# Re-planning the start of a fused attention and mixer kernel: TensorE transposes, GpSimd copies of V, single PSUM banks, row-tiled terms and zero products

## The chip, the cores and the metric

The kernel runs on one core of one Trainium2 chip. The metric is the device time of one execution in microseconds (us). Five engines share the work: TensorE (PE in the profile; its weight loads are PEld), VectorE (DVE), ScalarE (ACT), GpSimd (POOL) and SyncE (SP), with 16 DMA engines beside them. Each result below is the median of several executions, with the lowest and highest. The span is the time from the first to the last traced instruction of one execution; the time is 1.7 to 1.9 us longer than the span of the same execution.

## The reference

Attention over 4 batches, 8 heads, 768 positions and head size 64, with 8 global columns, a causal local window of 96 and a linear position bias, is followed by a low-rank token mixer and a two-layer channel network. Everything is float32 outside; the kernel works in float16 inside.

```python
keep = is_global | is_local                    # 8 global columns, 96 local ones
scores = np.where(keep, q @ k.T / 8 + bias, -1e9)
a = softmax(scores)
x = concat_heads(a @ v)                        # (4, 768, 512)
h = x.transpose(0, 2, 1) @ U @ V               # U: 768x32, V: 32x768
u = x + h.transpose(0, 2, 1)
out = u + np.maximum(u @ w_ch1, 0.0) @ w_ch2   # 512x2048, 2048x512
```

## The kernel before

Two heads of one batch make a pair, so there are 16 pairs, four in each batch. Batch 0 is pairs 0 to 3. A pair is loaded, its q and k are transposed, 128-column blocks of scores are formed and exponentiated, and multiplied with V. Since the window crosses block boundaries, the kernel holds k and V a second time, shifted by one block, as kO and vo (with the 8 global rows in front). Then the mixer makes uT of the pair. When four pairs are done, TensorE runs the channel products of that batch: M1 is the first (128 matmuls of 384 columns in each batch) and M2 the second. The attention of the next batch is slotted between them.

Every piece is a task with an assumed duration, a priority and dependences. A planner in the kernel's own Python simulates the engines with these durations and fixes each engine's order of instructions before the kernel is built. An engine then runs its instructions strictly in that order.

```python
PRIO = {"E012": 1443.3, "EX1.1": 338.0, ...}   # hand-found priorities of single tasks

# loads: all are issued by GpSimd, in the order k, q, v of each pair
tk = add(POOL, ldur, ..., ld(stgk, k, gk), after=prev, ...)
tq = add(POOL, ldur, ..., ld(stgq, q, gq), after=tk, ...)
tv = add(POOL, 1.04, ..., ldv, [c_zero], after=tq, ...)

# transposes: batch 0 by TensorE, all later pairs by DMA
if first:
    TK = add(PE, 0.38, base, tr(g1, stgk, gk), ...)          # 12 matmuls with an identity
    EK = add(ACT, 0.83, base + 1, evac(kT, gkT, g1, ACT), ...)
else:
    EK = add(SP, 0.35, base + 1, dtr(kT, gkT, stgk, gk), ...)  # dma_start(..., transpose=True)

# shifted V: batch 0 by DMA, all later pairs by VectorE
if eng == SP:
    nc.sync.dma_start(vof[32:P], vv[32:P, :, 0:NB - 1])
    for hi in range(2):
        nc.sync.dma_start(vof[0:NG, hi], vv[0:NG, hi, 0:1].broadcast_to((NG, NB - 1, D1)))
else:
    nc.vector.tensor_copy(vof, vv[:, :, 0:NB - 1])
    nc.vector.tensor_copy(vof[0:32], vv[0:32, :, 0:1].broadcast_to((32, 2, NB - 1, D1)))

# mixer: an aligned pair of PSUM banks; U products in 32-column tiles, h over all 128 rows
gx = Group("ps", n=2, among=A2)
nc.tensor.matmul(ps[R * g:R * g + R, gx.slot, 384:512], u16[:, c], xx[:, c], ...)
nc.tensor.matmul(ps[:, gx.slot + half, 0:HS], tmp[...], vrep[:, half * HS:(half + 1) * HS], ...)
# cast of x for the mixer: GpSimd for three of a batch's four pairs
XC = add(POOL, 0.83, base + 22, cast, [NM], acq=[gx16], ...)
...   # cut: scores, softmax, channel products, stores
```

The softmax here doesn't subtract the row's maximum and nothing guards it: scores larger than these inputs give would overflow.

Of the kernel before, what the change touches and what calls it, by code (L numbers as in the profile page):

```python
# [20 lines left out]
    "E012": 1443.3, "EX1.1": 338.0, "KO11": 1058.2, "NH3.1": 393.2, "PV2.1": 317.9, "PV9.2": 1009.0,  # L21
    "S0.0": -8.2, "S1.1": -12.6, "S11.1": 970.6, "S13.2": 1162.2, "S14.0": 1415.1, "S2.0": 228.3,
    "S3.1": 286.5, "S3.2": 282.8, "S4.0": 363.6, "S4.2": 398.6, "S5.0": 533.1, "TE6": 676.1,
    "X02": 262.7, "X06": 650.3, "mask1": 377.5, "mask2": 223.5, "mask4": 285.4, "mask7": 304.8,
}
CFG = {}
# [19 lines left out]
class Planner:  # L46
# [4 lines left out]
    def __init__(self, counts, dma_rate, hold):  # L51
        self.tasks, self.names = [], {}
        self.free = {k: [0.0] * n for k, n in counts.items()}
        self.dma_rate, self.hold = dma_rate, hold
# [9 lines left out]
    def pick(self, g):  # L64
        free = self.free[g.kind]
        best = None
        for i in g.among if g.among is not None else range(0, len(free) - g.n + 1, g.n):
            f = max(free[i:i + g.n])
            if f < 1e8 and (best is None or f < best[0]):
                best = (f, i)  # L70
        return best

    def run(self):
# [28 lines left out]
        while len(order) < len(self.tasks):  # L102
            best = None
            for e in engines:
                ready = []
                for t, r in live[e].items():
                    for g in t.acq:
                        if g.slot is None:
                            got = self.pick(g)
                            if got is None:  # L110
                                break
                            r = max(r, got[0])
                    else:
                        if t.size:
                            r = max(r, lanes[e][t.parts - 1])
                        ready.append((max(r, clock[e]), t.prio, t))
# [12 lines left out]
            if t.size:  # L129

                begin = max(t.end + 1.5, dma_free[t.eng])
# [6 lines left out]
                t.end += 0.4  # L138
# [4 lines left out]
            for g in t.acq:  # L143
                if g.slot is None:
                    g.slot = self.pick(g)[1]
                    for i in range(g.slot, g.slot + g.n):
                        self.free[g.kind][i] = 1e9
            for g in t.rel:
                g.readers -= 1
                g.free_at = max(g.free_at, t.end + 0.1)  # L150
                if g.readers == 0:
                    for i in range(g.slot, g.slot + g.n):
                        self.free[g.kind][i] = g.free_at
            order.append(t)
# [9 lines left out]
def kernel(  # L164
# [36 lines left out]
    def sb(name, shape, dt, n=None):  # L201
# [4 lines left out]
    ident = sb("ident", [P, P], FP32)  # L206
    ident16 = sb("ident16", [P, P], FP16)
    reli = sb("reli", [P, 256], I32)
    relb = sb("relb", [P, 256], FP32)
    rel3 = sb("rel3", [P, 384], FP32)  # L210
    mask = sb("mask", [P, H, 384], FP16)
    bias = sb("bias", [P, H, 384], FP16)
    uf = sb("uf", [P, NB, R], FP32)
    u16 = sb("u16", [P, NB, R], FP16)
# [26 lines left out]
        dma_rate=0.30e6,  # L241
# [3 lines left out]
    def add(eng, dur, prio, fn, deps=(), name="", **kw):  # L245
        return pl.add(name, eng, dur, PRIO.get(name, prio), fn, deps, **kw)

    ANY1, ANY2 = None, None
# [4 lines left out]
    c_ident = add(POOL, 0.6, -50, lambda: make_identity(nc, ident), name="ident")  # L253
    c_id16 = add(DVE, 0.35, -50, lambda: nc.vector.tensor_copy(ident16, ident), [c_ident], name="id16")
    c_iota = add(
        POOL, 0.35, -52,
        lambda: nc.gpsimd.iota(reli, pattern=[[1, 256]], base=0, channel_multiplier=-1), name="iota",
    )
    c_relf = add(DVE, 0.36, -51, lambda: nc.vector.tensor_scalar_mul(relb, reli, -1.0), [c_iota], name="relf")

    def causal():
        nc.gpsimd.affine_select(
            out=relb, in_=relb, compare_op=ALU.is_ge, fill=BIG,
            base=0, pattern=[[1, 256]], channel_multiplier=-1,
        )

    def window():
        nc.gpsimd.affine_select(
            out=relb, in_=relb, compare_op=ALU.is_ge, fill=BIG,
            base=NL - 1, pattern=[[-1, 256]], channel_multiplier=1,  # L270
        )

    c_sel1 = add(POOL, 0.41, -49, causal, [c_relf], name="sel1")
    c_sel2 = add(POOL, 0.41, -48, window, [c_sel1], name="sel2")

    def build_rel():
        nc.vector.tensor_copy(rel3[:, 128:256], relb[:, 128:256])
        nc.vector.tensor_copy(rel3[:, 256:384], relb[:, 0:128])
        nc.vector.tensor_copy(rel3[:, 0:128], relb[:, 0:128])
        nc.vector.tensor_scalar_max(rel3[0:NG, 0:256], rel3[0:NG, 0:256], float(-NL))  # L280

    c_rel = add(DVE, 0.97, -46, build_rel, [c_sel2], name="rel3")
# [18 lines left out]
    for h in range(H):  # L301
        e = ACT if h >= 1 else DVE
        c_bias.append(add(e, 0.54, -45 + h if h < 2 else 100 * (h // 2) - 30, bias_of(h, e), [c_rel], name=f"bias{h}"))

    def zero_fill():
        for i in range(N_V):
            nc.vector.memset(vo[i][0:32], 0.0)
            nc.vector.memset(vt[i][:, :, :, D:D1], 1.0)

    c_zero = add(DVE, 1.0, -60, zero_fill, name="zero")  # L310
# [3 lines left out]
    loads, c_w1, c_w2 = {}, [], []  # L314

    def add_load(p):
# [5 lines left out]
        def ld(dst, src, g):  # L322
            def go():
                if b == 0:
# [15 lines left out]
        ldur, parts = (0.72, 1) if b == 0 else (1.7, 2)  # L340
        lead = 60 if b == 0 else 160
        prev = loads[p - 1][5] if p else None
        tk = add(POOL, ldur, base - lead, ld(stgk, k, gk), after=prev, acq=[gk], size=0.39e6, parts=parts, name=f"lk{p}")
        tq = add(POOL, ldur, base - lead + 1, ld(stgq, q, gq), after=tk, acq=[gq], size=0.39e6, parts=parts, name=f"lq{p}")
        tv = add(POOL, 1.04, base - lead + 2, ldv, [c_zero], after=tq, acq=[gv], size=0.39e6, name=f"lv{p}")
        loads[p] = (gq, gk, gv, tq, tk, tv)

    def add_w1(i, prio):
# [4 lines left out]
                after=c_w1[-1] if c_w1 else loads[NP - 1][5], size=1.05e6, name=f"w1_{i}",  # L353
# [3 lines left out]
    def add_w2(i, prio):  # L357
# [4 lines left out]
                after=c_w2[-1] if c_w2 else c_w1[-1], size=1.05e6, name=f"w2_{i}",  # L362
# [4 lines left out]
    w2v = moe_w_ch2.rearrange("(c p) n -> p c n", p=P)  # L367
    for p in range(len(pairs)):
        add_load(p)
# [10 lines left out]
    c_mixl = add(SP, 0.9, -44, load_mixer, after=loads[0][3], size=0.2e6, parts=2, name="mixl")  # L380
    c_u16 = add(DVE, 0.3, 10, lambda: nc.vector.tensor_copy(u16, uf), [c_mixl], name="u16")
# [6 lines left out]
    c_vrep = add(SP, 1.3, 12, spread_v, [c_v16], size=0.15e6, parts=3, name="vrep")  # L388
# [4 lines left out]
    def attention(p):  # L393
# [3 lines left out]
        first = b == 0  # L397
        last = hp == NP - 1
# [34 lines left out]
        if first:  # L433
# [3 lines left out]
            ek, eq = CFG.get("EK", ACT), CFG.get("EQ", DVE)  # L437
            EK = add(ek, 0.83 if ek == ACT else 0.95, base + 1, evac(kT, gkT, g1, ek), [TK], acq=[gkT], rel=[g1], name=f"EK{p}")
            EQ = add(eq, 0.83 if eq == ACT else 0.95, base + 2, evac(qT, gqT, g2, eq), [TQ], acq=[gqT], rel=[g2], name=f"EQ{p}")
        else:  # L440
            EK = add(SP, 0.35, base + 1, dtr(kT, gkT, stgk, gk), [tk], acq=[gkT], rel=[gk], size=0.4e6, name=f"EK{p}")
            EQ = add(SP, 0.35, base + 2, dtr(qT, gqT, stgq, gq), [tq], acq=[gqT], rel=[gq], size=0.4e6, name=f"EQ{p}")
# [9 lines left out]

        KO = add(DVE, 0.5, base + 3, koff, [EK], name=f"KO{p}")

        def voff(eng):
            def go():
                vv, vof = vt[gv.slot], vo[gv.slot]
                if eng == SP:
# [8 lines left out]
        if first:  # L467
            VO = add(SP, 1.1, base + 4, voff(SP), [tv, c_zero], size=0.2e6, parts=3, name=f"VO{p}")
        else:
            VO = add(DVE, 0.6, base + 4, voff(DVE), [tv], name=f"VO{p}")  # L470
# [3 lines left out]
        for s in range(3):  # L474
            gsc = Group("ps", n=2, among=A2)
# [5 lines left out]
            def sc(s=s, gsc=gsc, lo=lo, biased=biased):  # L481
# [8 lines left out]
                for j in range(4):  # L490
                    i = 2 * s + j // 2
                    if j % 2 == 0 and i == 0:
                        continue
                    for hi in range(2):
# [8 lines left out]
                PE, (0.2 if s == 0 else 0.25) + ((0.33 if s == 0 else 0.43) if biased else 0), base + 5 + 3 * s, sc,  # L503
# [288 lines left out]
```

## Time and profile before

| | before |
|---|---|
| median of three timed runs | 254.1 us (253.96 to 254.72) |
| traced execution | 250.83 us, span 249.1 us |
| first M1 product that is part of a lasting run | 44.2 us |
| end of the last matmul | 245.6 us |
| busy over the span: TensorE, VectorE, ScalarE, GpSimd | 94, 44, 43, 32 % |

The page of the kernel before has one row for each engine, in 40 slices of 6.2 us, with the busy share in tenths; the PEclk row is the granted TensorE clock in tenths. The first line is the busy time of each engine, the last the chain that ended last, by engine.

```profile
PE 234.9 (94%) x1985; PEld 128.8 (52%) x1985; DVE 108.4 (44%) x222; ACT 106.4 (43%) x136; POOL 80.4 (32%) x101
PE   1979959999999999999999999999999999999994
PEclk9999986999999999999999999999999999999999
PE 83%; DMA 8%; ACT 3%; DVE 2%; POOL 1%; issue 1%; SPq 1%; POOLq 0%; DVEq 0%; ACTq 0%
```

TensorE is full after the seventh slice, so only the first 45 us can give anything. There the chain is on DMA for 8% of the span, and the clock falls in slices 6 and 7.

### The profile page before, as it was taken

What the parts mean: (1) busy time and instruction counts of PE and PEld (TensorE: products, weight loads), DVE (VectorE), ACT (ScalarE), POOL (GpSimd) and SP (SyncE); (2) the same over time, 40 slices, a digit from 0 to 9 for tenths busy, and PEclk for the clock granted to TensorE, in tenths of its full rate; (3) what the DMA queues carried; (4) which work ended last, traced back from release to release, by engine and by line L of the source; (5) the groups of instructions that cost most, each with busy time, mean ns of one, the idle gap of its engine ahead of it and who ended that gap; (6) DMA issues with size and microseconds to landing.
All of it is one profiled execution on the core that took longest, in us unless ns stands there. A gap on an engine that the chain in (4) does not pass through costs nothing.

```text
span 249.1 us, 4774 instructions
## 1 busy us (share of the span) xinstructions
PE 234.9 (94%) x1985; PEld 128.8 (52%) x1985; DVE 108.4 (44%) x222; ACT 106.4 (43%) x136; POOL 80.4 (32%) x101
## 2 busy tenths in 40 slices
PE   1979959999999999999999999999999999999994
PEld 1445535565544455655655445566544456654453
DVE  6445683241347885678875524443412110001221
ACT  2876915558404306777744202685510016650000
POOL 7956750492098491258660002001000000000000
PEclk9999986999999999999999999999999999999999
DMA  8999999999999999899994512000011220001112
GB/s 110 154 197 175 185 194 173 168 161 161 124 104 155 256 153 184 111 146 84 128 163 67 147 45 84 0 3 0 3 42 42 84 87 0 0 3 43 67 59 84
DMA packets 93877, 25.83 MB, mean 104 GB/s; under 512 B 83616, under 2 KB 90880, under 8 KB 93856
## 3 DMA queue, kind: packets, MB, share of 16 engines
q0 software_dynamic: 68864, 13.64, 65.9%
q1 hardware_dynamic: 24992, 11.90, 23.9%
q8 instruction: 15, 0.25, 0.4%
q14 instruction: 6, 0.05, 0.1%
HBM read 27.46 MB, written 6.29 MB: 136 GB/s over the span
## 4 chain that ended last, share of the span: by engine, by line
PE 83%; DMA 8%; ACT 3%; DVE 2%; POOL 1%; issue 1%; SPq 1%; POOLq 0%; DVEq 0%; ACTq 0%
PE ps L719 34%; PE ps L682 33%; DMA qT<-stgq 6%; PE ps L497 5%; PE ps L632 2%; PE ps L717 2%; DMA vo<-vt 2%; PE ps L566 2%; PE ps L640 2%; ACT ep L509 2%; PE ps L565 2%; PE ps L549 1%; PE ps L489 1%; ACT htr L699 1%; DVE kO L449 1%
## 5 line engine op out<-in xcount | busy, mean ns | idle before, releaser
L682 PE MATMUL ps<-uT,w 128*128 128x384 f16 x512 | 91.5, 329 | 1.6 <-DVE uT L658 1.1
L719 PE MATMUL ps<-w,htr 128*128 128x512 f16 (+1 forms) x400 | 88.6, 371 | 0.0
L699 ACT ACTIVATE htr<-ps 128x768 f16<-128x768 f32 x64 | 51.6, 810 | 61.0 <-PE ps L682 61.0
L509 ACT ACTIVATE ep<-ps 128x1024 f16<-128x1024 f32 (+1 forms) x48 | 44.8, 952 | 48.5 <-PE ps L497 48.2
L682 PEld LDWEIGHTS <-w 128*128 128x128 f16 x512 | 48.1, 98 | 33.1 <-issue 3.0
L719 PEld LDWEIGHTS <-htr 128*128 128x128 f16 x400 | 38.4, 98 | 40.9
L737 DVE TENSOR_TENSOR osb<-ps,x_sb 128x512 f32<-128x512 f32 (+1 forms) x25 | 16.7, 668 | 68.3 <-PE ps L719 68.3
L616 POOL CAST x<-x_sb 128x768 f16<-128x768 f32 x12 | 11.2, 934 | 87.4 <-DVE x_sb L601 87.4
L522 DVE TENSOR_TENSOR ep<-ep,mask 128x1024 f16<-128x1024 f16 x24 | 16.5, 687 | 17.1 <-ACT ep L509 17.0
L658 DVE CAST uT<-ps 128x384 f16<-128x384 f32 x28 | 14.6, 552 | 17.5 <-PE ps L640 17.5
L331 POOL DMA_DIRECT2D stgk<-in_k_dram x24 | 20.3, 868 | 0.0
L331 POOL DMA_DIRECT2D stgq<-in_q_dram x24 | 20.3, 867 | 0.0
L497 PE MATMUL ps<-qT,kT 64*128 64x128 f16 x192 | 16.9, 233 | 0.5 <-DVE qT L422 0.4
L335 POOL DMA_DIRECT2D vt<-in_v_dram x16 | 17.0, 1063 | 0.0
L566 PE MATMUL ps<-vt,ep 128*128 128x65 f16 x192 | 16.0, 196 | 0.6 <-DVE uT L658 0.3
L566 PEld LDWEIGHTS <-ep 128*128 128x128 f16 x192 | 13.6, 99 | 4.1 <-issue 0.9
L497 PE MATMUL ps<-qT,kO 64*128 64x128 f16 x160 | 14.9, 234 | 0.6 <-DVE kO L449 0.6
L601 DVE TENSOR_TENSOR x_sb<-ps,rcp 128x768 f32<-128x768 f32 x16 | 15.2, 956 | 0.5
L565 PE MATMUL ps<-vo,ep 128*128 128x65 f16 x160 | 14.3, 196 | 0.7 <-DMA vo<-vt 0.7
L497 PEld LDWEIGHTS <-kO 64*128 64x128 f16 x160 | 7.8, 100 | 11.0 <-issue 8.8
L565 PEld LDWEIGHTS <-ep 128*128 128x128 f16 x160 | 11.7, 100 | 1.8 <-DMA vo<-vt 0.6
L497 PEld LDWEIGHTS <-kT 64*128 64x128 f16 x192 | 9.9, 101 | 5.2 <-issue 4.9
(54 smaller groups left out, 149.6 us busy)
## 6 DMA issues: line engine op xcount, KB each, us to landing
out_dram<-osb SPq DMA_DIRECT2D x23, 256.0 KB, 2.0
w<-in_moe_w_ch_dram POOLq DMA_DIRECT2D x8, 512.0 KB, 10.8
vt<-in_v_dram POOLq DMA_DIRECT2D x16, 192.0 KB, 5.6
stgk<-in_k_dram POOLq DMA_DIRECT2D x24, 96.0 KB, 5.6
stgq<-in_q_dram POOLq DMA_DIRECT2D x24, 96.0 KB, 4.5
stgk<-in_k_dram POOLq DMA_DIRECT2D x4, 192.0 KB, 4.7
stgq<-in_q_dram POOLq DMA_DIRECT2D x4, 192.0 KB, 5.1
vo<-vt SPq DMA_DIRECT2D x4, 121.9 KB, 6.5
```

Of the source, the lines that this page charges most:

```text
L331: nc.gpsimd.dma_start(o[:, :, hi], src[b, h0 + hi].rearrange("(n p) d -> p n d", p=P))
L335: nc.gpsimd.dma_start(vt[gv.slot][:, :, :, 0:D], v[b, h0:h0 + 2].rearrange("h (n p) d -> p h n d", p=P),)
L497: nc.tensor.matmul(t[:, hi, j * P:(j + 1) * P], lhs, qt[r, i * P:(i + 1) * P], start=not biased, stop=True, skip_group_check=biased,)
L509: nc.scalar.activation(ep[gep.slot][:, :, lo:512], ps[:, gsc.slot:gsc.slot + 2, lo:512], AF.Exp, scale=qk_scale)
L522: nc.vector.tensor_tensor(ev, ev, mv, ALU.mult)
L565: nc.tensor.matmul(o, e[:, hi, j * P:(j + 1) * P], vof[:, hi, i - 1], start=True, stop=False)
L566: nc.tensor.matmul(o, e[:, hi, (j + 1) * P:(j + 2) * P], vv[:, hi, i], start=(i == 0), stop=True)
L601: nc.vector.tensor_tensor(xo, pvo()[:, :, :, 0:D], rcp[p % 2].unsqueeze(3).broadcast_to((P, 2, NB, D)), ALU.mult)
L682: nc.tensor.matmul(ps[:, g.slot + half, 0:HS], w1[:, dc, jt * P:(jt + 1) * P], ub[:, dc, half * HS:(half + 1) * HS], start=(dc == 0), stop ...
L699: nc.scalar.activation(htr[:, jt].rearrange("p (h c) -> p h c", h=2), ps[:, g.slot:g.slot + 2, 0:HS], AF.Relu)
L719: nc.tensor.matmul(o, htr[:, jc, tt * P:(tt + 1) * P], w2[:, jc, c0:c1], start=False, stop=(jc == NJC - 1),)
L737: nc.vector.tensor_tensor(osb[go.slot][:, c0:c1], ps[:, g.slot, 0:c1 - c0], xb[:, tt, c0:c1], ALU.add)
```

## The change

It wants TensorE to start its lasting run of channel products earlier. It replaces what stood on the chain by work of engines: V's shifted copy goes from DMA to GpSimd, the q and k of pairs 4 and 5 from DMA transpose to TensorE. It feeds TensorE products of zeros where the plan has it wait, to keep its clock up. It lets the mixer take two single PSUM banks in place of an aligned pair, and cuts mixer terms to 32 rows, so that two can run side by side. Loads are issued in another order, the planner's durations are new, and so are the priorities. Cut to its core (cuts are marked):

```diff
-PRIO = { "E012": 1443.3, ... 24 entries }
-CFG = {}
+PRIO = { "E010": 1127.6, ..., "VO0": 46.0, ..., "lk5": 306.3, "lv2": 22.4, "w1_0": 323.2, ... 20 entries }
+CFG = {'petr': (4, 5), 'bias_dve': (0, 2)}
...  # in batch 0, v of a pair is now issued after k and q of the next pair
+        then = add_load(p)
+        if p < NP:
+            if late:
+                late()
+            late = then
...  # transposes
-        if first:
+        if p in by_pe:              # pairs 0 to 5
...  # shifted V in batch 0
+                if eng == POOL:
+                    nc.gpsimd.tensor_copy(vof, vv[:, :, 0:NB - 1])
+                    nc.gpsimd.tensor_copy(vof[0:32], vv[0:32, :, 0:1].broadcast_to((32, 2, NB - 1, D1)))
...  # mixer banks
-        gx = Group("ps", n=2, among=A2)
+        gx = [Group("ps", among=A1), Group("ps", among=A1)]
...  # h products on 32 rows each; u16 now holds four copies of U
+            for half in (1, 0):
+                r = slice(R * half, R * half + R)
+                nc.tensor.matmul(
+                    ps[:, gx[half].slot, 0:HS], tmp[b % 2][r, hp * P:(hp + 1) * P],
+                    vrep[r, half * HS:(half + 1) * HS], start=False, stop=True, skip_group_check=True)
...  # the three value products of a pair become one task; M2's first terms two at a time on 32 rows;
...  # M2 in four chunks; the mask's distance table is built by VectorE, not GpSimd
+    def idle(n, width, bank):       # zero products, up to the first M1
+        for _ in range(n):
+            nc.tensor.matmul(ps[:, bank, 0:width], zero16[:, 0:P], zero16[:, 0:width], start=True, stop=True)
```

## The prediction

> **What bounds the kernel now.** I read the chain that ended last first, because busy shares cannot tell who waits. Its merged form for the first 45 us holds two single pieces that no engine works in (columns: start us, duration us, what):
>
> ```profile
> 9.53 5.01 DMA vo<-vt
> ...
> 24.90 13.87 DMA qT<-stgq
> 38.77 0.04 issue
> 38.81 0.93 PE ps L497 x14
> ```
>
> The first is the copy of V's shifted blocks by DMA for pair 0, the second the DMA transpose of q for pair 4: its scores stand in TensorE's queue ahead of the mixer and of the first channel products. Together they are 18.9 us of the chain. After 45 us it is TensorE almost alone.
>
> Second, the table of stretches (stretch, us, then busy us of PE, PEld, DVE, ACT, POOL, then the granted clock and DMA):
>
> ```profile
> 5.20:21.70 16.50, 14.47 (x145) 7.64 (x147) 7.41 (x19) 10.44 (x18) 13.92 (x18) 1.00 1.70 175
> 21.70:35.30 13.60, 11.69 (x200) 6.98 (x196) 10.49 (x23) 9.68 (x13) 8.54 (x11) 1.00 1.42 185
> 35.30:42.20 6.90, 6.01 (x43) 3.09 (x43) 2.59 (x8) 2.10 (x3) 0.74 (x1) 0.51 1.94 172
> 42.20:45.00 2.80, 2.65 (x29) 1.70 (x28) 1.38 (x2) 2.61 (x4) 0.00 (x0) 1.00 1.24 203
> 45.00:245.60 200.60, 200.03 (x1577) 109.39 (x1575) 82.77 (x161) 80.34 (x98) 53.26 (x61) 1.00 0.78 90
> ```
>
> TensorE is full from 45 to 245.6 us, and the clock is halved from 35.3 to 42.2. The 1.00 of the first stretch is a default (the records begin at 21.7 us), which the timeline of matmuls shows: pairs of score matmuls start 0.10 us apart early and 0.056 us apart later.
>
> ```profile
> 9.90 0.31 PE L497 MATMUL ps<-qT,kT 64*128 64x128 f16 x2
> 10.00 0.31 PE L497 MATMUL ps<-qT,kO 64*128 64x128 f16 x2
> 10.11 0.31 PE L497 MATMUL ps<-qT,kT 64*128 64x128 f16 x2
> ...
> 76.31 0.22 PE L497 MATMUL ps<-qT,kT 64*128 64x128 f16 x2
> 76.37 0.22 PE L497 MATMUL ps<-qT,kO 64*128 64x128 f16 x2
> 76.42 0.22 PE L497 MATMUL ps<-qT,kT 64*128 64x128 f16 x2
> ```
>
> So TensorE runs at half speed for the first 21.7 us too. Full-clock work between 5.2 and 45 us, from starts in the saturated part: 20 channel matmuls at 0.1625 (3.25), bias products 8 x 0.1625 + 16 x 0.216 (4.8), 8 transpose sets of 0.36 (2.9), 55 score pairs at 0.056 (3.1), 102 value products at 0.030 (3.1), mixer terms U 4 x 0.30, transposes 24 x 0.056, h 8 x 0.1625 (3.8), some 4.1 of mode switches (below): 25.0 us. The stretch lasts 39.8, so 14.8 us are lost to waits and half clock. The span is thus 5.2 + 25.0 + 14.8 + 200.6 + 3.5 of tail (last matmul to end) = 249.1. The timed median is 254.1, 5.0 above the traced span; I keep that 5.0.
>
> **What the Trainium skill says.** "TensorE: Matmul & The Clock Gate", Part 1: the array starts at half clock and is released after about 3.4 us of sustained activity, and one idle window throttles it again. The trace agrees: 0.105 against 0.056 us as shown, and throttling at 35.3 after TensorE had stood still 1.1 us around 32 and again 1.1 us before 35.98. That products of zeros count as activity the page does not state for this gate, and no run yet shows it.
> "TensorEngine Tiling (Array Packing)", Key Properties: a change of tiling mode drains the array. The trace agrees: 8 products of 512 columns take 8 x 0.216 = 1.73 us, yet the next scores (64-row tiles) start 1.84 us after the first, and leaving them costs the same:
>
> ```profile
> 74.41 1.90 PE L719 MATMUL ps<-w,htr 128*128 128x512 f16 x8
> 76.25 0.23 PE L497 MATMUL ps<-qT,kO 64*128 64x128 f16 x2
> ```
>
> That is 0.095 us each way; no gap stands before value products, which keep the mode.
> "DMA: Bandwidth & Descriptors", Issuing engines are not separate DMA queues: all run on the same 16 engines. The page's DMA row is at 8 or 9 tenths in slices 1 to 20 (to 125 us), so early transfers queue: v of pair 3, issued at 11.83, lands at 20.95.
> "GPSIMD Engine Reference", Key points: GpSimd shares its SBUF interfaces with VectorE's two-port modes. The trace agrees: the 128x160 kO copy takes 0.18 us alone and 0.82 beside GpSimd's work at 17.2 us.
>
> **The change part by part.**
> V copied by GpSimd (batch 0): removes four times three DMAs and the 5.0 us on the chain. GpSimd's 128x768 cast lasts 0.82 us, so two copies of 650 columns are about 1.5 us (estimate). v of pair 0 is issued after k, q of pair 1, so it lands near 10.5 us rather than 7.75; the first value product can start near 12.3 instead of 14.58 for the shifted blocks. Gain here some 2 us, and GpSimd gets 6 us more work.
> q, k by TensorE for pairs 4, 5: removes four DMA transposes, hence the 13.9 us wait, and larger packets shorten four loads. Adds 4 transpose sets, 4 x 0.36 plus up to 4 x 0.19 of switches: +2.0 us of TensorE. ScalarE gets 4 evictions of 0.81, 3.3 us.
> Zero products: fill waits until the first channel product, from about 2 us. The array should be warm by 6 to 8 us instead of 21.7, and not throttled at 35.3. They take no time that is needed, except where data come earlier than planned.
> Row-tiled mixer terms: two h products side by side take 0.1625 plus two switches, 0.35, against 0.325. U full width is 6 x 0.056 = 0.34 against 0.30 with its own switches. Two first terms side by side take 0.216 + 0.19 = 0.41 against 0.43. So instead of saving half they earn nothing: 16 x (0.03 + 0.03) = +1.0 us.
> Start: a memset (about 0.45) and the iota (0.38) now stand before k's first load on GpSimd; first data at 5.9 instead of 5.2 us, +0.7.
> PSUM by single banks, merged value products and four chunks of the second product cost nothing where TensorE is full.
>
> When can continuous channel products start? Transfers: v of pair 3 near 20.5 (estimate from 20.95, with the V copies gone and the later start); then k, q, v of pair 4 and k of pair 5 (1.1, 1.1, 1.6, 1.1) and the first weight slice (3.5): about 29 us. ScalarE in batch 0: 4 k evictions of 0.81, exps of 2.85 per pair, 6 biases of 0.52, one uT 0.5, 18.3 us from 6.6, so about 25 at the earliest; pair 3's tail after its last exp some 3 us: 28. VectorE is as full. So 29 to 31, against 44.2 for the first lasting run before.
>
> Sum: 5.9 + 25.0 + 200.6 + 3.0 (2.0 + 1.0 added) + 3.5 = 238.0, plus what is still lost. Loss I estimate at 4.5 (14.8 before): 1.2 for the first 2.4 us at half clock, 2.0 for batch 0's dependences, 1.3 in the first channel product, where ScalarE has 16 relus of 0.81, two pairs of exps, evictions and masks (24 us) beside TensorE's 25. Span 242.5, time 247.5 us.
>
> **The rivals.** (1) Zero products do not warm the array, or come at the wrong times. For: plans miss by microseconds under DMA queueing; 14.5 busy us of 16.5 did not release it before. Against: those were half idle by spacing. Then batch 0's TensorE work of some 20 us runs partly at half speed: +4 to 5, time 252. (2) A new bound in batch 0: GpSimd carries V copies, loads and casts, its copies stretch VectorE's, and channel products start at 34 instead of 30: time 251. (3) Everything fits the plan: no loss but the cold start, and the drains half hidden by neighbours that switch anyway: span 238.5, time 243.5. (4) The transfers were hidden anyway: refuted, since 13.9 us of transpose stand on the chain and TensorE is full behind it.
>
> **Range and chances.** From 243.8 (rival 3) to 251.5 (rivals 1 or 2), middle 247.5. Two per cent below 254.1 is 249.0, only 1.5 us above the middle, so faster 0.70, same 0.28, slower 0.02: a slowdown would have to lose more than the wait removed.
>
> **What would show it.** Right: score pairs 0.056 us apart before 10 us; no halved stretch after; no vo or qT DMA of pair 4 on the chain; the first lasting channel run near 30 us; h products starting together but with 0.095 us gaps on both sides; TensorE's saturated part ending 3.5 us before the end. Wrong: a halved clock beyond 12 us, VectorE or GpSimd on the chain of batch 0 for over 5 us, weights landing after 32 us, or row-tiled terms without drains (then some 3 us faster).

## The result, and the profile after

| | before | after |
|---|---|---|
| median, beside each other (4 runs each) | 254.41 us (253.96 to 255.03) | 245.12 us (244.77 to 245.38) |
| traced execution, time and span | 250.83, 249.1 | 245.38, 243.6 |
| first M1 product; the last of the 128 in batch 0 | 35.98; 64.45 | 32.25; 61.24 |
| end of the last matmul | 245.6 | 240.2 |

The kernel is faster: the ratio is 0.963, with a 95% interval from 0.961 to 0.966. Ratios here are the mean time of one kernel's fast runs over that of the other's in the same rounds, so they are not quite the ratio of the medians quoted beside them. Executions over 1.5% slower than the fastest of the same kernel are left out of the means.

The same rows of the page of the kernel after (slices of 6.1 us), with its chain by engine:

```profile
PE 234.9 (96%) x2096; PEld 130.2 (53%) x2096; DVE 107.2 (44%) x222; ACT 109.2 (45%) x139; POOL 81.9 (34%) x106
PE   6799999998999999999999999999999999999994
PEclk9999999999999999999999999999999999999999
PE 74%; DMA 13%; POOL 9%; issue 2%; DVE 0%; POOLq 0%
```

The busy time of TensorE is the same 234.9 us by chance: the after kernel has 111 more matmuls, among them zero products, but none of its real work runs at half clock. A "busy" TensorE in the first five slices includes the zero products, and so isn't proof of useful work. The chain has changed hands: ScalarE and VectorE are off it and GpSimd is on it for 9%.

The chain of the kernel after over its first 45 us (start us, duration us, what) shows where:

```profile
4.60 6.98 DMA vt<-in_v_dram
...
11.72 0.79 POOL vo L502
12.57 0.72 POOL vo L503
...
24.40 0.66 POOL stgk L345
25.05 1.51 POOL w L381 x2
...
30.11 11.78 DMA vt<-in_v_dram
...
44.65 13.36 DMA stgq<-in_q_dram
```

Neither vo<-vt nor qT<-stgq stands there as a transfer, as they did before. In their place GpSimd copies V, issues loads, casts, and waits for loads before it can issue more. TensorE doesn't appear in it at all before 45 us (the next wait for GpSimd's cast, at 60 us, leads the chain there): as the trace has it, this stage hangs on one engine's list and on the landings that it waits for. A chain doesn't say how much removing it would give. TensorE stands close behind: from 32.25 to 60 us it idled only in the three gaps that are described below, 2.7 us together from one matmul's start to the next.

The table of stretches of the kernel after (stretch, us, busy us of PE, PEld, DVE, ACT, POOL with counts, granted clock, DMA share, GB/s):

```profile
5.50:10.20 4.70, 3.47 (x66) 2.78 (x66) 4.18 (x10) 2.98 (x6) 4.70 (x9) 1.00 1.43 153
22.00:28.00 6.00, 5.82 (x100) 3.62 (x98) 4.33 (x9) 5.53 (x8) 5.33 (x9) 1.00 0.87 83
28.00:34.00 6.00, 5.98 (x88) 4.21 (x83) 5.02 (x16) 3.88 (x8) 5.64 (x7) 1.00 1.23 201
40.00:240.10 200.10, 198.29 (x1583) 108.07 (x1583) 79.91 (x160) 80.51 (x98) 50.00 (x58) 1.00 0.77 92
```

The POOL column is 4.70 of 4.70, 5.33 of 6 and 5.64 of 6. In the second line the transfers fall to 83 GB/s, less than half of the 201 that follow. In the trace no transfer starts from about 23.8 to 25.7 us: GpSimd, which issues these loads, was copying and casting and issued none between 19.62 and 24.35 us. The first weight slice, issued at 25.05, lands at 31.74.

The answers to the score pairs of before are these two lines of TensorE's timeline in the kernel after:

```profile
11.19 0.22 PE L554 MATMUL ps<-qT,kO 64*128 64x128 f16 x2
11.24 0.22 PE L554 MATMUL ps<-qT,kT 64*128 64x128 f16 x2
```

Pairs of score matmuls start 0.056 us apart at 11 us already. The clock record says full clock from 4.19 us to the end.

And these lines answer the drain. They are from the last M2 block of the kernel after (start, duration, line, tile shapes, count); L781 is the pair of 32-row first terms:

```profile
235.74 0.59 PE L787 MATMUL ps<-w,htr 128*128 128x512 f16 x2
236.27 0.28 PE L781 MATMUL ps<-tmp,vrep 32*128 32x256 f16 x2
236.48 3.67 PE L787 MATMUL ps<-w,htr 128*128 128x256 f16 x32
```

Two terms of 256 columns that start together cost 0.21 us of the queue (236.27 to 236.48), where side by side they would take 0.109 without a gap. For 512 columns the medians are 0.312 us from the last M2 product to the terms and 0.317 from the terms to the next product, against 0.216 within a run of M2 products: 0.096 and 0.101 of gap.

What loss is left after 32 us sits in three gaps: 39.6 us (0.8, the load of q for pair 5), 47.5 (0.6), and 58.6 (1.4, of which 1.1 idle). The last is worth a look, since it comes back in many experiments. First GpSimd's timeline of the kernel after, with the wait before an instruction and what ended it in brackets:

```profile
56.39 0.82 POOL L351 DMA_DIRECT2D stgk<-in_k_dram  x1 [3.52 <-DMA w<-in_moe_w_ch_dram]
57.49 1.64 POOL L351 DMA_DIRECT2D stgq<-in_q_dram  x2 [0.27 <-DMA stgk<-in_k_dram]
59.11 0.84 POOL L687 CAST x<-x_sb 128x768 f16<-128x768 f32 x1
```

Then the producer of the cast's input on VectorE in the same kernel:

```profile
55.57 0.96 DVE L666 TENSOR_TENSOR x_sb<-ps,rcp 128x768 f32<-128x768 f32 x1
```

And TensorE, which waits for the cast:

```profile
60.01 0.51 PE L606 MATMUL ps<-ident,x 128*128 128x128 f16 x6 [1.07 <-POOL x L687]
```

The input was ready at 56.53 us. The cast began at 59.11, because it stands behind load issues in GpSimd's order, and before the first of these GpSimd had stood idle 3.52 us, in a wait for a weight slice that landed at 55.45. TensorE ran dry 1.07 us.

### The profile page after: what moved, and what is told of

Read it like the earlier page. It is cut to its first block, busy times and chain, and to the rows that moved or that the text cites. A ratio compares the mean times of both kernels' runs of the same rounds, so it can differ in the third digit from the quotient of the medians.

```text
span 243.6 us, 4964 instructions
## 1 busy us (share of the span) xinstructions
PE 234.9 (96%) x2096; PEld 130.2 (53%) x2096; DVE 107.2 (44%) x222; ACT 109.2 (45%) x139; POOL 81.9 (34%) x106
## 4 chain that ended last, share of the span: by engine, by line
PE 74%; DMA 13%; POOL 9%; issue 2%; DVE 0%; POOLq 0%
PE ps L787 35%; PE ps L739 26%; DMA vt<-in_v_dram 8%; DMA stgq<-in_q_dram 5%; PE ps L554 3%; PE ps L781 2%; PE ps L606 2%; PE ps L628 2%; PE ps L611 2%; PE ps L627 1%; POOL w L381 1%; POOL vo L502 1%; PE ps L702 1%; POOL vo L503 1%; POOL stgq L345 1%
## 5 line engine op out<-in xcount | busy, mean ns | idle before, releaser
L739 PE MATMUL ps<-uT,w 128*128 128x384 f16 x512 | 88.9, 326 | 0.0
L739 PEld LDWEIGHTS <-w 128*128 128x128 f16 x512 | 47.7, 98 | 31.8 <-issue 1.0
L787 PEld LDWEIGHTS <-htr 128*128 128x128 f16 x400 | 36.7, 98 | 41.3 <-issue 3.4
L687 POOL CAST x<-x_sb 128x768 f16<-128x768 f32 x12 | 11.2, 932 | 60.7 <-DVE x_sb L666 60.7
L579 DVE TENSOR_TENSOR ep<-ep,mask 128x1024 f16<-128x1024 f16 x24 | 16.9, 713 | 13.2 <-ACT ep L566 13.0
L351 POOL DMA_DIRECT2D stgk<-in_k_dram x20 | 16.7, 844 | 7.8 <-DMA w<-in_moe_w_ch_dram 3.5
L351 POOL DMA_DIRECT2D stgq<-in_q_dram x20 | 16.6, 838 | 4.6 <-DMA vt<-in_v_dram 1.6
L554 PE MATMUL ps<-qT,kT 64*128 64x128 f16 x192 | 15.1, 218 | 0.3 <-DVE x_sb L666 0.3
L628 PEld LDWEIGHTS <-ep 128*128 128x128 f16 x192 | 12.5, 97 | 2.1 <-DMA stgk<-in_k_dram 0.2
L628 PE MATMUL ps<-vt,ep 128*128 128x65 f16 x192 | 13.4, 193 | 0.0
L554 PE MATMUL ps<-qT,kO 64*128 64x128 f16 x160 | 13.4, 219 | 0.0
L627 PE MATMUL ps<-vo,ep 128*128 128x65 f16 x160 | 12.0, 193 | 0.0
L695 DVE CAST tmp<-ps 128x128 f16<-128x128 f32 x16 | 4.7, 291 | 15.7 <-PE ps L611 15.6
```

Of the source, the lines that this page charges most:

```text
L351: nc.gpsimd.dma_start(o[:, :, hi], src[b, h0 + hi].rearrange("(n p) d -> p n d", p=P))
L554: nc.tensor.matmul(t[:, hi, j * P:(j + 1) * P], lhs, qt[r, i * P:(i + 1) * P], start=not biased, stop=True, skip_group_check=biased,)
L579: nc.vector.tensor_tensor(ev, ev, mv, ALU.mult)
L628: nc.tensor.matmul(o, e[:, hi, (j + 1) * P:(j + 2) * P], vv[:, hi, i], start=(i == 0), stop=True)
L739: nc.tensor.matmul(ps[:, g.slot + half, 0:HS], w1[:, dc, jt * P:(jt + 1) * P], ub[:, dc, half * HS:(half + 1) * HS], start=(dc == 0), stop ...
L787: nc.tensor.matmul(o, htr[:, jc, tt * P:(tt + 1) * P], w2[:, jc, c0:c1], start=False, stop=(jc == NJC - 1),)
```

## The experiments

Twelve runs follow, two of them of the unchanged kernels, all of them with the right result. Runs of the first eight shared one chip, whose runs of the before kernel have a median of 252.68 us (252.1 to 254.6, 10 runs); the last four shared another, with 252.0 (250.26 to 254.71, 11 runs). These are lower than the 254.41 above, while the after kernel repeats within 0.4 us (245.12 and 245.50). So I compare variants with the after kernel by their own times, and with the before kernel by the ratio on the same chip. In four of the runs that undo a part (a_dmat, a_vodma, a_oldplan, a_pairbank) the measured time lies above both of the ranges that had been expected.

### The kernel before, unchanged (b_again)

No edit. It tests how much of the difference is the spread of the kernel before, and whether 5.0 us between traced span and median is a constant.

> The kernel before once more, unchanged. It settles the 5.0 us that I took as the difference between timed median and traced span. In the changed kernel's runs that difference is 1.7 us (245.38 against a span of 243.6). Theory: it is 1.7 us here too, so the ordinary run of before has a span near 252.4 and the trace of 249.1 that I worked from was an unusually short run; the missing 3.3 us are about one more throttled window of 6.83 us at half clock, so spans of about 252 with a granted clock of 0.97 or less against 0.986. Rival: the traced run was ordinary and the difference is a constant 5 us of this program; then spans of 249 to 249.5 at 0.986 beside times of 254.

Measured: 253.02 us (251.7 to 254.76, 4 runs), ratio 1.000 (0.994 to 1.006). The traced execution took 254.76 us with a span of 253.0, a difference of 1.76. For the trace that the prediction used it is 250.83 - 249.1 = 1.73, and for the kernel after 245.38 - 243.6 = 1.78. So the 5.0 was wrong: that trace had caught a short execution, and the rest is inside the span. Two stretches of b_again (columns as in the table above):

```profile
16.30:23.10 6.80, 6.17 (x59) 3.01 (x58) 2.88 (x7) 2.42 (x4) 4.21 (x6) 0.50 1.73 174
36.70:47.00 10.30, 7.77 (x48) 3.87 (x48) 4.11 (x10) 3.24 (x4) 0.77 (x2) 0.50 1.71 181
```

Here the clock was already full from 12.9 to 16.3 us, was halved again, and the later half-clock stretch lasted 10.2 us in place of 6.8. The lasting run of M1 began at 48.1 us, 3.9 later than in the first trace, and the span is 3.9 longer. The kernel before, which starves its TensorE, doesn't have one time but a spread of them: 4.8 us over all its runs, against 1.5 over the ten of the kernel after. Whether the longer half-clock stretch made the execution longer or came from the same waits, this run can't tell.

### Without the zero products (a_nowarm)

```diff
-CFG = {'petr': (4, 5), 'bias_dve': (0, 2)}
+CFG = {'petr': (4, 5), 'bias_dve': (0, 2), 'warm': False}
```

> The changed kernel without its zero products, same order of everything else. Theory (the clock matters): TensorE stays at half speed until 15 to 20 us and may be throttled again later, first lasting channel run 4 to 6 us later, time 249 to 251. Rival (the removed transfers are the whole gain, batch 0 is set by transfers and ScalarE anyway): 245 to 246.

Measured: 245.46 us (244.91 to 245.65), ratio 0.972 (0.970 to 0.974): as fast as the kernel after, within 0.4 us. TensorE's timeline in this run shows that the clock did stay down longer:

```profile
13.49 0.32 PE L554 MATMUL ps<-qT,kO 64*128 64x128 f16 x2
13.60 0.32 PE L554 MATMUL ps<-qT,kT 64*128 64x128 f16 x2
...
14.79 0.22 PE L554 MATMUL ps<-qT,kO 64*128 64x128 f16 x2
14.84 0.22 PE L554 MATMUL ps<-qT,kT 64*128 64x128 f16 x2
```

Pairs are 0.11 us apart until 14.5 us and 0.055 after. Still M1 begins at 32.86 us (32.25 with zeros), and the last M1 of batch 0 is at 61.55 (61.24). Ten microseconds at half clock cost some 0.3 us, which is within the noise: TensorE was not what the stage waited for. And nothing throttled later, with no zeros to prevent it: the longest stops had gone with the other parts. So in the changed kernel the theory that the early clock matters falls. About the half clock after 35 us in the kernel before this run says nothing; there a_dmat and b_pe45 bear on it. The traced a_dmat had full clock from 5.06 us on and was as slow as the kernel before, and the traced b_pe45 had full clock from 23.3 us on, yet its lasting run came no earlier.

### Pairs 4 and 5 by DMA transpose again (a_dmat)

```diff
-CFG = {'petr': (4, 5), 'bias_dve': (0, 2)}
+CFG = {'petr': (), 'bias_dve': (0, 2)}
```

> The changed kernel with pairs 4 and 5 transposed by DMA again; the plan knows the longer transfers now and places their scores later. Theory (the 13.9 us transpose wait was the larger of the two waits): the scores still hold up TensorE or later pairs, 248 to 251. Rival (with a plan that knows the transfer, the wait is hidden behind channel products): 244 to 246.5, as 2 us of TensorE transposes go.

Measured: 253.21 us (251.67 to 254.98), ratio 1.003: 8.1 us slower than the kernel after, and the whole gain is gone. The first M1 starts at 38.22. A line of this run's TensorE timeline, the piece of its chain at that time, and the issue of the transpose of q for pair 4 with the time that it took to land:

```profile
31.38 4.97 PE L825 MATMUL ps<-zero 128*128 128x128 f16 x86
...
31.44 4.91 PE ps L825 x86
...
26.23 2.15 SPq L469 DMA_TRANSPOSE qT<-stgq  x1
...
DMA to landing us min/median/max: 5.7/5.7/5.7
```

The scores of pair 4, which stand ahead of M1 in the order, run from 36.28 on, right when the 86 zero products end. But the transposed q had landed at 31.96 us, so this isn't the transfer wait of 13.9 us that the prediction named. The zeros stand on the chain themselves: the plan had set a long wait aside for the transpose and filled it with a fixed number of zeros, and on the chip these held TensorE for some 2 to 4 us after the data were there. The prediction had allowed for this: zeros cost nothing "except where data come earlier than planned". Nor does this delay last: the last M1 of batch 0 falls at 61.62, only 0.4 later than in the kernel after. Then four gaps of 0.8 to 2.2 us at 88 to 98 us, in which the chain runs through VectorE and ScalarE and not through a transfer, set TensorE back again, and the M1 of batch 2 starts at 152.0 in place of 145.4. That later delay is the one that stays. So the run shows that this plan falls apart without the part, and not that 8.1 us is what waiting for the transfers costs.

### V's shifted copy by DMA again (a_vodma)

```diff
-CFG = {'petr': (4, 5), 'bias_dve': (0, 2)}
+CFG = {'petr': (4, 5), 'bias_dve': (0, 2), 'VO': 'SSSS'}
```

> The changed kernel with V's shifted blocks of batch 0 copied by DMA again. Theory: the first value products wait for the copy behind the loads in the queues, 246.5 to 248. Rival: GpSimd was the bound of batch 0 (busy 5.3 of 6 us between 22 and 28 us) and its copies stretched VectorE's kO copies (one took 1.55 us), so freeing it gives as much as the transfer costs: 244 to 246.

Measured: 249.70 us (249.13 to 250.33), ratio 0.989 (0.986 to 0.991): 4.6 us slower than the kernel after. GpSimd was freer, and the first weight slice landed at 25.9 us in place of 31.74, yet M1 started at 36.56. Twice 28 zero products stand on the chain, with 1.67 us each. They too held TensorE: the data that the product after the first block waits for had landed at 22.25 us, 4.1 us before it ran, and what the first M1, right after the second block, waits for at 25.92. The copies by GpSimd pay in this plan, although they delay the weights by almost 6 us, but up to 3.3 of the 4.6 us may be zeros that a wrong forecast had put there. No run undid V or the transposes without the zeros, so this rival is untested. In this run M1 stood behind attention and zeros in the order and did not wait for its weights, which were there more than 10 us earlier; in the kernel after the two come together, the weights 0.5 us before M1.

### The kernel before with zero products (b_warm)

```diff
+    c_wz = add(POOL, 0.5, -99, lambda: nc.gpsimd.memset(zero16, 0.0), name="wz")
...  # idle() and its calls as in the change, with the old plan
```

> The kernel before with zero products alone added, in the gaps that its own plan foresees. New theory, after the run without zero products lost nothing: transfers and evictions set batch 0, so a warm array early is worth nothing, 251.5 to 254; only the throttled 10 us after 36 us, where TensorE has channel products to do, could give 2 to 4 us, if a product happens to stand in that wait, which the old plan does not foresee. Rival (half clock is a cause of the time before): 247 to 250.

Measured: 253.77 us (250.94 to 256.59, 4 runs), ratio of the fast runs 1.001 (0.996 to 1.007). The profiled run, 256.59, counts as slow, so I don't use its length. In it the clock was still halved at 15.4 and at 42.7 us, since the plan's idle times and the real ones differ: a zero product at a planned pause doesn't help in an unplanned one (TensorE stood still 2.6 us at 13.2 and 4.0 at 39.6). Zeros alone gain nothing. Since they didn't keep the clock up, the run doesn't tell what a full clock would have given.

### The kernel before with TensorE transposes for pairs 4 and 5 (b_pe45)

```diff
-                if b == 0:
+                if p < 6:
...
-        if first:
+        if p < 6:
```

> The kernel before with q and k of pairs 4 and 5 transposed by TensorE, nothing else. Theory (the transpose wait on the chain is the larger part): 247 to 249.5. Rival (the V copy's 5 us and the queueing behind it only move the wait; one transfer in its place holds up TensorE): 251 to 253.

Measured: 252.21 us (251.13 to 255.33), ratio 0.997 (0.995 to 1.000), a gain of about 0.5 us that is hardly clear of noise. The 13.9 us piece of the chain was removed and almost nothing came of it (up to 46 us the largest shares of the chain are now ScalarE's exponentials with 13.6% and the DMA of vo with 13.4%): the first M1 is at 38.47, and its lasting run at 44.96, no earlier than before (44.16). A theory that sums up what a part takes off the chain falls with this run.

### The kernel before with both parts (b_vo_pe45)

```diff
...  # as b_pe45, and
+                if eng == POOL:
+                    nc.gpsimd.tensor_copy(vof, vv[:, :, 0:NB - 1])
+                    nc.gpsimd.tensor_copy(vof[0:32], vv[0:32, :, 0:1].broadcast_to((32, 2, NB - 1, D1)))
...
-            VO = add(SP, 1.1, base + 4, voff(SP), [tv, c_zero], size=0.2e6, parts=3, name=f"VO{p}")
+            VO = add(POOL, 1.5, base + 4, voff(POOL), [tv, c_zero], name=f"VO{p}")
```

> The kernel before with both transfers replaced (V copies of batch 0 by GpSimd, q and k of pairs 4 and 5 by TensorE), without zero products, single banks, row tiles or the retuned plan. Theory (the two waits are the gain): 244.5 to 247. Rival (the retuned plan with measured durations carries half of it): 248 to 251.

Measured: 250.12 us (248.31 to 250.92), ratio 0.990 (0.985 to 0.994), a gain of 2.6 us. The lasting run of M1 starts at 41.97, and a half-clock stretch stands from 31.8 to 42.0 us. The two parts that removed the waits on the chain give a third of the gain. The rest must come from how everything else is arranged, or from parts that pay only together, which the last set tests.

### Mixer terms over all 128 rows (a_norow)

```diff
+    def spread_u():
+        nc.vector.memset(u16, 0.0)
+        for c in range(NB):
+            nc.vector.tensor_copy(u16[:, c, c % RG], uf[:, c])
...
-                r = slice(R * half, R * half + R)
+                r = slice(0, P)
...
-                                r = slice(R * n, R * n + R)
+                                r = slice(0, P)
```

Each chunk of U sits in its own row group with zeros in the others, so the sum over all 128 rows gives the same terms as before the change. The tasks and the orders are the same.

> The changed kernel with the mixer's terms over all 128 rows (each row group holds a partial sum as before, same order of tasks, same number of products), so no change of tiling mode. Theory (0.095 us of drain on each side eats the gain): 244.3 to 245.5, that is 0 to 0.8 us less than the changed kernel's 245.1. Rival (two products side by side save one in each pair): 16 x 0.1625 + 13 x 0.216 = 5.4 us more, 249.5 to 251.

Measured: 244.51 us (244.11 to 245.40), ratio 0.969 (0.966 to 0.971), span 242.8. The start-to-start medians around these terms are 0.216 and 0.162 us, the bare time of 512 and 384 columns: the gaps are gone, and with them the parallel start. The run is 0.6 us below the kernel after, and 0.95 below a_nowarm on the same chip, whose interval it touches. So two tiles side by side earn nothing, and may cost up to 1 us.

### The kernel after, again (a_again)

No edit.

> The changed kernel itself, as the reference for the three runs beside it on the same chip: 244.7 to 245.5, as in its first four runs.

Measured: 245.50 us (244.66 to 246.16, 6 runs), ratio 0.972 (0.968 to 0.977), traced span 244.4. On this chip the gain over the kernel before is 6.5 us, in the first comparison it was 9.3; the difference is in the kernel before.

### The operations kept, the old order of loads and no hand-found priorities (a_oldplan)

```diff
-PRIO = {
+PRIO = {}
+PRIO_ = {
...
-        if p < NP:
-            if late:
-                late()
-            late = then
-            if p == NP - 1:
-                late()
-        else:
-            then()
+        then()
```

> The changed kernel with two pieces of its plan undone and every operation kept: V of a pair is loaded right behind its own q (as before, not behind the next pair's k and q), and the list of tuned priorities is empty. Theory (both waits alone gave the old kernel only 2.6 us, so the order of issue carries the rest): the first lasting channel run comes 3 to 5 us later than 32.3, time 248.5 to 250.5. Rival (the operations carry the gain, the order is noise): 244.5 to 246.5.

Measured: 253.02 us (251.87 to 254.30), ratio 1.004: 7.5 us slower than the kernel after on the same chip. All operations of the change are in it, and nothing of its gain. GpSimd's timeline in this run:

```profile
53.75 1.64 POOL L352 DMA_DIRECT2D stgk<-in_k_dram  x2 [0.90 <-DMA stgq<-in_q_dram]
55.38 0.88 POOL L681 CAST x<-x_sb 128x768 f16<-128x768 f32 x1
```

And TensorE's:

```profile
56.31 0.51 PE L600 MATMUL ps<-ident,x 128*128 128x128 f16 x6 [2.31 <-POOL x L681]
```

The input of this cast was ready at 51.37 us; it waited 4.0 us behind load issues. One stall of 2.3 us was 1.07 in the kernel after, and half clock follows it from 57.2 to 60.7 us. M1 starts at 35.32, its longer runs at 39.52, and the last M1 of batch 0 is at 67.95 in place of 61.24, so most of the loss arises in batch 0. The run undoes two things at once, the place of V in the load order and the priorities, so it doesn't divide the 7.5 us between them.

### The mixer's banks as an aligned pair again (a_pairbank)

```diff
-        gx = [Group("ps", among=A1), Group("ps", among=A1)]
+        gx2 = Group("ps", n=2, among=A2)
+        gx = [gx2, Half(gx2)]
```

> The changed kernel with the mixer's two PSUM banks taken together as an aligned pair, as before, instead of one by one. Theory (PSUM holds up batch 0 little): 245 to 246. Rival (banks are short in batch 0 and later beside the channel products, so tasks move): 246.5 to 248.

Measured: 249.57 us (248.54 to 250.48), ratio 0.988 (0.983 to 0.994): 4.1 us slower than the kernel after. M1 starts at 32.91, almost as early (32.25). The loss comes later: gaps at 27.3 (0.8), 39.0 (1.3), and at 57, where TensorE waits 2.46 us for the same late cast (its input was ready at 55.37, it began at 58.90); a stretch of half clock follows from 60.3 to 63.7 us, and the last M1 of batch 0 is at 65.58 in place of 61.24. Each mixer task took two banks before and after, so the difference lies in what the planner could order when.

### An attempt at a better kernel (a_best)

```diff
-PRIO = { ... 20 entries }
+PRIO = { ... 48 entries, searched with the planner }
-    c_wz = add(POOL, 0.5, -99, lambda: nc.gpsimd.memset(zero16, 0.0), name="wz")
+    c_wz = add(DVE, 0.6, -99, lambda: nc.vector.memset(zero16, 0.0), name="wz")
...  # k of pair 0 issued before the iota; mixer terms over 128 rows as in a_norow
-    done, until = c_wz.end + 0.3, pl.names["M1a0.0"].start
+    done, until = c_wz.end + 0.3, 9.0
```

> A version meant to beat both: full-height mixer terms, k of pair 0 issued before the iota with the zeros written by VectorE (first data some 0.8 us earlier), zero products only in the first 9 us, and priorities searched anew with durations corrected for the drains. Theory (the loss left is the late first data, the drains and two waits for transfers): 242 to 244. Rival (what is left is TensorE's work plus waits that the plan does not foresee): 244.3 to 246.

Measured: 248.67 us (247.77 to 249.52, 6 runs), ratio 0.985 (0.980 to 0.989): 3.2 us slower than the kernel after. The searched plan promised some 2 us less than the plan of the kernel after. On the chip TensorE stood idle for 1.8 us at 43.5 and for 3.4 us at 55.5 us, the second again for GpSimd's cast, which began at 58.40 behind a load issue that had itself waited 3.47 us for a weight slice. The planner's forecast is not good enough to choose between plans that differ by 2 us: run by itself, it puts the end of the last store of the kernel after at 235.5 us (the span was 243.6), and the start of M1 in the kernel before at 33.1 (a lasting run from 44.2).

## Why the prediction was right or wrong

The time, 247.5, was 2.4 us above the measured 245.12, inside the range. The verdict (faster, at 0.70) was right. The miss is of the offset: 5.0 us between span and time was 3.2 too high (1.78 measured), and the span 1.1 too low (242.5 against 243.6), which took back a part of it. With the right offset the prediction would have been 242.5 + 1.78 = 244.3, 0.8 us low. There is luck in this: the span came out near although the value of several parts was wrong, as the list shows. (Two slips in the prediction: the range starts at 243.8, though rival 3, which it names, gives 243.5; and the first product with the shifted blocks of before starts at 13.96 us, 14.58 is the second.)

**The bound before.** That the first 45 us hold all that can be gained was right: after 40 us the kernel after has TensorE busy 198.29 of 200.10 us. That two pieces of DMA on the chain were the cause was right only in part: replacing the transposes in the kernel before gives 0.5 us (b_pe45), both pieces 2.6 (b_vo_pe45). Undoing either part in the changed kernel costs 8.1 (a_dmat) and 4.6 us (a_vodma), but in the first 45 us of these runs zero products of the plan stand on the chain where it stalls, and not these transfers.

**Start.** 5.9 us was predicted, the first real matmul is at 5.50. The memset and the iota lasted 0.48 and 0.33 us, about as thought, but k's load was issued only 0.34 us later than before (1.59 against 1.25), and lands at 5.46.

**Zero products.** The prediction said warm by 6 to 8 us and no later throttling. The clock is full from 4.19 us and stays so. The step that failed is the value: the loss of 14.8 us was put on "waits and half clock" together, and rival 1 gave half clock 4 to 5 us. a_nowarm measures 0.3 to 0.4 in the changed kernel. The page "TensorE: Matmul & The Clock Gate" in Part 1 puts the ramp's penalty under 1% of a typical span; 0.4 of 245 us is under 0.2%. One reading in the prediction is too strong: it puts the throttling at 35.3 us to one idle window and says that the trace agrees. TensorE wasn't idle for such a window. It was busy 1.76 of the 3.41 us before, and 2.00 of 3.41 in b_again, with stops of about 1 us among other work.

**V by GpSimd.** Predicted: first value product near 12.3 us, a gain of 2. Measured: v of pair 0 landed at 11.59 (10.5 predicted), and the first product with the shifted blocks is at 15.95, later than before, although the copy of pair 0 ended at 13.29. The new order puts the transposes and scores of pair 1 (13.85 to 15.9 us) ahead of it. Undoing the part costs 4.6 us in this plan all the same, up to 3.3 of it zero products. Removing a wait for pair 0 was thus not where the worth lies; why the part is worth so much was not isolated.

**q, k by TensorE for pairs 4 and 5.** The wait of 13.9 us is gone from the chain, but it was worth 0.5 us alone, and a_dmat doesn't bring it back: there q's transpose took 5.7 us, and what held TensorE was the 86 zeros. The cost of +2.0 us of TensorE was not measured by itself.

**Row-tiled terms.** Predicted to earn nothing, +1.0 us, from 0.095 us of gap each way. Measured gaps 0.096 and 0.101, and 0.6 to 0.95 us less without tiles. This step was right.

**"PSUM by single banks, merged value products and four chunks … cost nothing where TensorE is full."** This is the step that failed most. It treated the re-planning as free of effect. The single banks are worth 4.1 us (a_pairbank), the order of loads with the priorities 7.5 (a_oldplan). The four undone parts add up to 8.1 + 4.6 + 4.1 + 7.5 = 24.3 us, against a gain of 6.5 to 9.3. Parts of a plan don't add: what one is worth depends on the plan around it. One caution belongs to these numbers: in each variant the planner orders everything anew, with priorities that were found for the full change. The cost of an undone part thus includes a plan that no longer fits, and in a_dmat and a_vodma the zeros that this plan put in the wrong place.

**M1's start and the loss left.** Predicted 29 to 31 us, measured 32.25; weights at 29, measured 31.74. This is rival 2's mechanism, GpSimd as the new bound, at about half its size (it said 34 in place of 30). One of the prediction's own signs of being wrong came true here: it named GpSimd on the chain of batch 0 for over 5 us, and before 32.25 us the chain has 18.8 us of GpSimd. The traces that speak for it are the chain, which consists of GpSimd and of what it waits for, and the 1.9 us in which no transfer started. VectorE was slowed too. Two lines of its timeline in the kernel after, of the same copy alone and beside GpSimd's work:

```profile
19.07 0.19 DVE L491 COPY kO<-kT 128x160 f16<-128x160 f16 x1
...
21.49 1.55 DVE L491 COPY kO<-kT 128x160 f16<-128x160 f16 x1
```

The second copy began at 21.49 us, just after one of GpSimd's V copies (21.44 to 22.16), and ended at 23.04, after GpSimd's next instruction too, a cast that ended at 22.94.

The loss was estimated as 3.2 us before the first channel product's stage and 1.3 in it, the latter by ScalarE. By difference (240.2 - 5.5 - 228.6 of work, the last as predicted and not measured) 6.1 us were lost; 2.7 of them are the three gaps after 32 us (0.78, 0.55 and 1.39 from one matmul's start to the next), so some 3.4 lie before. The early size was about right, with hardly any clock in it; the later was twice the estimate, and stands behind a transfer, VectorE and GpSimd's cast, not behind ScalarE.

**What stays open.** No run moved the cast or the load issues to another engine, so that GpSimd's order sets the rest is not proved by an undo. It is read from five traces (the kernel after, a_norow, a_oldplan, a_pairbank, a_best), in which TensorE waits 1.1 to 3.4 us for a cast (0.95 in a_again and only 0.26 in a_nowarm, at no gain in time); in the three of them whose VectorE timeline I read there (after, a_oldplan, a_pairbank), the cast's input had been ready for 2.6, 4.0 and 3.5 us. What the old load order and the priorities are each worth is not known either, nor what the undone parts cost without zero products.

## What to carry to other kernels

A wait on the chain is worth what stands next behind it: taking 13.9 us off the chain gave 0.5 us alone, while undoing the same part in the new plan cost 8.1, so test a part both by adding it to the old kernel and by taking it from the new one, and look in the trace at what then stands on the chain. Filler work of fixed length, such as zero products, holds its engine when the data come earlier than planned. On an engine that works its list in order, don't put a small piece of work that others wait for behind load issues that wait for a landing or a buffer. And before a traced span is turned into a time, compare the traced execution's own time with the median: the kernel before varied by 4.8 us from one execution to another.

## What the Trainium skill lacked or had wrong

- "TensorE: Matmul & The Clock Gate", Part 1, doesn't say whether products of zeros release this gate. They do: full clock from 4.19 us with them, from 14.5 us without.
- The same page gives the release as about 4 us into sustained activity, within 500 ns. It doesn't say how much a later half-clock stretch varies between executions of a kernel whose TensorE pauses. In two executions of the kernel before, half clock after 30 us lasted 6.83 and 10.24 us, and the spans were 249.1 and 253.0 us; b_warm, a_oldplan and a_pairbank each have a stretch of 3.41 us.
- "TensorEngine Tiling (Array Packing)", Key Properties, states that a change of mode drains the array, with no figure. Here it is 0.096 us on entry and 0.101 on leaving, which eats the gain of two 512-column products side by side (0.216 us).
- "SBUF — State Buffer", Who interferes with whom, says that whoever issues first has the shared port pair for its whole instruction while the other blocks. It doesn't say whether the blocked one can lose twice running. One 128x160 VectorE copy that reads like it went from 0.19 to 1.55 us, over two GpSimd instructions of 0.72 and 0.82 us.
- No page that I read puts a figure to a GpSimd cast held behind load issues in its own order: 1.07 us of idle TensorE in the kernel after, 2.31, 2.46 and 3.43 in three variants.
